# Decay times v in three wide bf16 matmuls per head, with three PSUM slots per output, in an mLSTM and gated-FFN kernel

## The chip, the cores and the metric

The kernel runs on one core of one Trainium2 chip. The metric is the device time of the kernel in microseconds, the median over runs. Names of engines: TensorE (PE) multiplies, with its weight loads listed apart (PEld); VectorE (DVE), ScalarE (ACT) and GpSimd (POOL) work on tiles; SyncE (SP) issues most transfers.

## The reference, cut to what matters

There are 4 batches of 8 heads, 768 steps and a head width of 40. Per step:

```python
m_new  = max(f + m, i);  f_stab = exp(f + m - m_new);  i_stab = exp(i - m_new)
C = f_stab * C + i_stab * outer(v, k);  n = f_stab * n + i_stab * k
y = sigmoid(o_gate) * (C @ q) / max(|n . q|, 1)
```

The 3072 rows of y (320 wide) go through a gated FFN of width 1536: `(sigmoid(x @ w_gate) * (x @ w_val)) @ w_out`.

## The kernel before, in words

The recurrence is done in 6 chunks of 128 steps. A *unit* n is one chunk c of one batch b, n = 4c + b, with all 8 heads, so there are 24 units. In a unit the scores (`s`, lines 694, 757 and 812) are multiplied by a decay matrix d (`t`, L876), and the product, 128x128 per head, is multiplied by v with a column of ones appended, 41 columns (`av`). From chunk 1 on the state's part (`in`, L918; `ti`, L923) is added. The output is then normed (`nd`, L955 to L957), gated (`ns`, L961), scaled (`ro`) and split into a high and a low part for the FFN (`xh`, `xl`). `cs`, `cd`, `cm` and `ca` (L1013 to L1056) carry the state on.

Units 0 to 7 multiply decay by v in float32 (L942). From unit 8 on, 16 units in all, both operands are split into bf16 pieces: decay into its upper half, a rest's upper half and a last rest (`da`, `db`, L891 and L895, on POOL), v likewise (`va`, `vb`, L902 and L906, on POOL). Six products of pieces are summed in PSUM:

```python
dp = top(dm[n]) if i == 0 else top(dr[n][0]) if i == 1 else dr[n][1]
vp = [top(vt[n])] if i == 2 else [top(vt[n]), top(vr[n][0]), vr[n][1]][: 3 - i]
for h in range(H):
    for j, w in enumerate(vp):
        nc.tensor.matmul(pv_[n][:, h, :], dp[:, h, :], w[:, h, :], ...)
```

That is 6 matmuls of 41 columns for each of 8 heads, 48 a unit (L935), each with its own load of decay as the weights. One VectorE instruction, `ad` (L950, 328 elements a row), then adds the state's part in place.

The FFN (`ffn`, L1064 to L1125) works through tiles of 256 or 512 columns of x. `u` and `r` (L1075, L1079, L1080) make two PSUM tiles, `pg0` and `pg1`, one buffer each. `th` and `gx` gate them, `gh` and `gl` split the result, and `dn` (L1112 to L1114) multiplies by w_out into four PSUM tiles `po`. The tiles n = 16 to 39, among them those that go with units 8 to 11, are of 256 columns.

Scores, `in`, `av`, `cs` and the transposes share two PSUM tiles, `pa0` and `pa1`, taken in turn in the order of the program (`pst`, tag "pa"). An instruction that takes one waits until everything that reads its last content is done.

The order of all work is a list written out by hand, `ORDER`. `emit` goes through it, and each engine gets its instructions in that order and keeps it. So what stands before a late instruction on its own engine is done, and what stands behind it waits. SyncE issues transfers in the same order. `wk` and `wm` (L408, L398) are matmuls on zeros that fill TensorE's time at the start.

Of the kernel before, what the change touches and what calls it, by code (L numbers as in the profile page):

```python
# [23 lines left out]
    'AV': 2,  # L24
# [7 lines left out]
    'AD': 1,  # L32
# [15 lines left out]
    i2 lf wdr0 li i3 wz tab wk0 war0 pz wk1 wk2 wk3 wdo0 ga i0 iz gm0 il sp0.0 lq2 i1 wdv0 gs0 wbr0 gb wao0 wbo0 lq0  # L48
    wav0 lk0 gc tap tac sp0.1 ee0.0 lk1 gm1 sp1.0 wco0 lq1 wcr0 ee0.1 kw0 lo0 tr0.1 wor0 whr0 wbv0 wlr0 gm2 lv0 i5
    tr0.0 sp1.1 cp0.0 cp0.1 s0.0 tr1.0 woo0 wdo4 gm3 lo1 ee1.0 ee1.1 cp1.0 wdo1 ld2 l10 tr1.1 kw1 wcv0 wov0 t0.0 lv1  # L50
    lq3 wdg0 cp1.1 wao4 tr2.0 l11 cp2.0 s1.0 who0 gm4 cs0 wlo0 wbo4 wco4 t0.1 whv0 av0 t1.0 og1 wlv0 og0 cm0.1 t1.1
    lk2 wao1 ld3 wbo1 woo4 ee2.1 who4 wco1 wlo4 woo1 wk4 av1 ee2.0 wdg1 em2 nd0 ns0 gs1 wk5 cm0.0 ro0 wk6 wdo3 wag0
    nd1 ns1 tr3.0 cp3.0 xd0 wbg0 lk3 lv2 l12 tr2.1 xt0 cp2.1 ro1 wcg0 kw2 ee3.1 wk7 xh0 wk8 who1 wk9 gm5 xd1 i8 wk10
    lo2 xt1 wdr1 wog0 xh1 xl0 wk11 xl1 wag1 ld4 wdv1 wbg1 wm gd s2.0 t2.0 t2.1 whg0 u1.0 r1.0 wlo1 tbp tbc wlg0
    tr3.1 lq4 wao3 wbo3 cp3.1 ee3.0 u0.0 r0.0 war1 og2 em3 lv3 kw3 lo3 th0 wco3 wcg1 woo3 wdo5 cs1 wbr1 cm1.1 who3
    wlo3 lk4 wog1 gx0 cm1.0 whg1 gh0 lq5 av2 ns2 ee4.0 u0.1 ee4.1 gl0 r0.1 th1 dn0.0 nd2 l13 wcr1 ro2 s3.0 wor1 t3.0
    t3.1 wlg1 u1.1 r1.1 wav1 wbv1 cs2 wcv1 wdv3 wao5 wbo5 u0.2 wov1 xd2 cm2.1 tr4.0 wco5 cm2.0 em4 cp4.0 gx1 whv1
    wlv1 whr1 wlr1 woo5 gh1 wdo2 gl1 dn0.1 og3 qb4.0 xt2 av3 ns3 dn1.1 xh2 nd3 dn1.0 u1.2 xl2 ro3 r0.2 th2 r1.2 gx2
    wao2 wbo2 xd3 tdp wco2 wdo10 tdc lk5 tr4.2 cp4.2 u0.3 gh2 r0.3 xt3 tr4.1 gl2 u1.3 r1.3 lo4 woo2 qb4.2 wao10 i6
    th3 xh3 xl3 who2 gs3 gx3 u0.4 r0.4 who5 s4.0 cp4.1 gh3 gs5 kw4 gl3 wlo5 tr5.0 wav3 t4.0 ld5 cp5.0 u1.4 r1.4  # L60
    wbo10 lv4 og4 wlo2 th4 dn2.1 dn3.1 dn2.0 dn3.0 gx4 u0.5 wbv3 ee5.0 wcv3 wco10 qb4.1 gh4 gl4 woo10 s4.2 u1.5 r0.5
    wov3 r1.5 t4.2 who10 wdv2 wlo10 whv3 dn4.2 lv5 cs3 wlv3 wdg2 th5 wag2 gx5 cm3.1 gh5 l14 wdr2 in4 wbg2 wav2 u0.6
    ti4 r0.6 gl5 cm3.0 dn5.2 wcg2 th6 wbv2 dn4.3 s4.1 wcv2 u1.6 wog2 r1.6 war2 wov2 u0.7 qb5.0 wbr2 wcr2 ee5.1 t4.1
    gx6 r0.7 whv2 wdg4 lk6 whg2 wlv2 gh6 dn5.3 gl6 em5 av4 cs4 wor2 lq6 gs4 th7 wdr3 wdg3 u1.7 r1.7 wlg2 whr2 lo5
# [33 lines left out]
    r1.32 ea11 dn31.3 gx32 gh32 gl32 u0.34 dn31.2 r0.34 tq12 lq13 tw12.3 tw12.0 tw12.1 cm9.0 tw12.2 u1.34 lo11 xw9.3
    r1.34 dn32.3 th34 gx34 u0.33 va11 r0.33 dn32.2 ee11 em11 gh34 gl34 u1.33 sh11.1 r1.33 ob1.1 sl11.0 lv12 th33
    gx33 av10.0 ld13 sl11.1 av10.1 av10.2 u0.35 xr8.1 kw11 r0.35 gh33 cd9.1 og11 gl33 ad10 xr9.0 ns10 cd9.0 s11.2  # L100
    t11.2 dn33.3 dn33.2 nd10 u1.35 r1.35 s11.0 dn34.3 t11.0 lq15 vb11 th35 gx35 dn34.2 gh35 ro10 cs10 lk13 xr9.2
    s11.1 sr12.10 ca9.1 u0.36 sr12.00 ea12 r0.36 ee12 em12 cm10.1 th36 gl35 u1.36 ca9.0 t11.1 da11 tx10 xw10.1
# [83 lines left out]
    dn102.3 ob5.3 dn102.2 ob5.2  # L186
# [11 lines left out]
def mlstm_then_gated_ffn_kernel(  # L198
# [158 lines left out]
    @op("i3")  # L357
    def _():
        block_mask(bmask, L)

    @op("i4")
    def _():
        block_mask(cmask, DA)

    @op("i5")
    def _():
        nc.gpsimd.tensor_copy(rmask, bmask[:, :, 0])
# [799 lines left out]
```

## Time and profile before

| | us |
|---|---|
| median of 3 runs | 517.56 |
| the three runs | 517.18, 517.56, 519.47 |
| the profiled execution | 516.09 |
| its span, first to last instruction | 514.3 |
| lies around the span | 1.8 |

The rows further down come from the profiled execution. A duration of one matmul (mean ns) holds its way through the array, and matmuls overlap: the pace of a stream is read from the chain of waits, where a piece of so many instructions has the length by which it moved the end on.

### The profile page before, as it was taken

What the parts mean: (1) busy time and instruction counts of PE and PEld (TensorE: products, weight loads), DVE (VectorE), ACT (ScalarE), POOL (GpSimd) and SP (SyncE); (2) the same over time, 40 slices, a digit from 0 to 9 for tenths busy, and PEclk for the clock granted to TensorE, in tenths of its full rate; (3) what the DMA queues carried; (4) which work ended last, traced back from release to release, by engine and by line L of the source; (5) the groups of instructions that cost most, each with busy time, mean ns of one, the idle gap of its engine ahead of it and who ended that gap; (6) DMA issues with size and microseconds to landing.
All of it is one profiled execution on the core that took longest, in us unless ns stands there. A gap on an engine that the chain in (4) does not pass through costs nothing.

```text
span 514.3 us, 11007 instructions
## 1 busy us (share of the span) xinstructions
PE 505.0 (98%) x4020; PEld 467.1 (91%) x4021; DVE 328.6 (64%) x699; ACT 242.4 (47%) x560; POOL 247.8 (48%) x273
## 2 busy tenths in 40 slices
PE   6999999999999999999999999999999999999997
PEld 4799988889999999998988888998888888999996
DVE  8888777775776677676766456766545474642332
ACT  4888766554444354645343543343344324233322
POOL 3656446567147687469635544287315504510000
PEclk9999999999999999999999999999999999999999
DMA  8999775339798797799879787699465735220000
GB/s 200 281 226 238 204 194 141 105 94 176 139 185 156 176 208 152 168 203 173 168 130 165 191 155 144 139 180 187 103 138 104 166 87 114 64 56 5 1 27 27
DMA packets 222478, 74.17 MB, mean 144 GB/s; under 512 B 167380, under 2 KB 214168, under 8 KB 222424
## 3 DMA queue, kind: packets, MB, share of 16 engines
q1 hardware_dynamic: 221336, 73.20, 65.3%
q8 instruction: 32, 0.52, 0.4%
q10 hardware_dynamic: 1088, 0.26, 0.2%
q14 instruction: 22, 0.18, 0.1%
HBM read 61.54 MB, written 11.90 MB: 143 GB/s over the span
## 4 chain that ended last, share of the span: by engine, by line
PE 94%; DMA 2%; ACT 2%; SPq 0%; DVE 0%; issue 0%; DVEq 0%
PE pg L1075 39%; PE po L1112 9%; PE po L1114 8%; PE po L1113 8%; PE pg L1079 7%; PE pg L1080 6%; PE av L935 4%; PE in L918 2%; PE s L757 2%; PE av L942 2%; PE cs L1018 2%; PE s L812 1%; DMA d<-mscr 1%; DMA st_v<-in_moe_w_val_dram 1%; ACT d L639 1%; PE s L694 1%
## 5 line engine op out<-in xcount | busy, mean ns | idle before, releaser
L1097 ACT ACTIVATE gh<-pg 128x256 fp32r<-128x256 f32 (+1 forms) x103 | 48.3, 469 | 141.9 <-DVE pg L1092 116.7
L1092 DVE SCALAR_TENSOR_TENSOR pg<-sg,pg 128x256 f32<-128x256 f32 (+1 forms) x103 | 54.8, 532 | 92.4 <-PE pg L1080 74.7
L1075 PE MATMUL pg<-xh,wh 128*128 128x256 f32 (+1 forms) x412 | 104.5, 334 | 0.1
L1075 PE MATMUL pg<-xh,wl 128*128 128x256 f32 (+1 forms) x412 | 100.4, 325 | 0.0
L1075 PE MATMUL pg<-xl,wh 128*128 128x256 f32 (+1 forms) x412 | 100.2, 324 | 0.0
L1112 PE MATMUL po<-oh,gh 128*128 128x320 f32 x288 | 92.8, 322 | 0.0
L1114 PE MATMUL po<-oh,gl 128*128 128x320 f32 x288 | 89.1, 309 | 0.0
L1113 PE MATMUL po<-ol,gh 128*128 128x320 f32 x288 | 88.9, 309 | 0.0
L1085 ACT ACTIVATE sg<-pg 128x256 f32<-128x256 f32 (+1 forms) x103 | 48.2, 468 | 72.6 <-PE pg L1080 71.2
L1102 DVE TENSOR_TENSOR gl<-pg,gh 128x256 fp32r<-128x256 f32 (+1 forms) x103 | 54.4, 528 | 36.6 <-ACT gh L1097 34.9
L1075 PEld LDWEIGHTS pg<-xl,wh 128*128 128x128 f32 x412 | 68.5, 188 | 7.4 <-POOL xl L1008 0.3
L1075 PEld LDWEIGHTS pg<-xh,wl 128*128 128x128 f32 x412 | 68.6, 188 | 7.1
L1075 PEld LDWEIGHTS pg<-xh,wh 128*128 128x128 f32 x412 | 67.5, 188 | 3.5 <-DVE gl L1102 0.7
L1079 PE MATMUL pg<-xh,w 128*128 128x256 f32 (+1 forms) x206 | 68.2, 332 | 0.0
L1080 PE MATMUL pg<-xl,w 128*128 128x256 f32 (+1 forms) x206 | 66.7, 324 | 0.0
L1112 PEld LDWEIGHTS po<-oh,gh 128*128 128x128 f32 x288 | 54.1, 188 | 2.8 <-ACT gh L1097 0.2
L1113 PEld LDWEIGHTS po<-ol,gh 128*128 128x128 f32 x288 | 54.2, 188 | 2.6
L1114 PEld LDWEIGHTS po<-oh,gl 128*128 128x128 f32 x288 | 54.0, 188 | 0.5 <-DVE gl L1102 0.4
L675 POOL TENSOR_SCALAR_AFFINE_SELECT d<-d 128x1024 f32<-128x1024 f32 x22 | 26.0, 1182 | 52.9 <-ACT d L671 52.1
L891 POOL TENSOR_TENSOR dr<-d 128x1024 f32<-128x1024 f32 x16 | 30.4, 1899 | 34.8 <-DVE d L876 34.4
L876 DVE TENSOR_TENSOR d<-s,d 128x384 f32<-128x384 f32 (+2 forms) x68 | 35.0, 528 | 15.8 <-PE s L757 9.2
L1080 PEld LDWEIGHTS pg<-xl,w 128*128 128x128 f32 x206 | 38.7, 188 | 2.7
(160 smaller groups left out, 883.1 us busy)
## 6 DMA issues: line engine op xcount, KB each, us to landing
d<-mscr SPq DMA_DIRECT2D x22, 512.0 KB
ks<-scq SPq DMA_DIRECT2D x48, 168.0 KB
qs<-scq SPq DMA_DIRECT2D x48, 168.0 KB
scq<-tq SPq DMA_DIRECT2D x64, 80.0 KB
su_o<-in_moe_w_out_dram SPq DMA_DIRECT2D x12, 320.0 KB
o<-in_o_gate_dram SPq DMA_DIRECT2D x24, 160.0 KB
v<-in_v_dram SPq DMA_DIRECT2D x24, 160.0 KB
out_dram<-ob SPq DMA_DIRECT2D x24, 160.0 KB
```

Of the source, the lines that this page charges most:

```text
L876: nc.vector.tensor_tensor(y, ps_[n, g][:, :nh, :], y, ALU.mult)
L891: E("da", n).tensor_tensor(dr[n][0], dm[n], top(dm[n]), ALU.subtract)
L1075: nc.tensor.matmul(p, w[y][:, a, fs], x[c][:, a, n0:n1], start=(i + a == 0), stop=False)
L1079: nc.tensor.matmul(pg[n, y], w2[y][:, fs], xh[c][:, 2, n0:n1], start=False, stop=False)
L1080: nc.tensor.matmul(pg[n, y], w2[y][:, fs], xl[c][:, 2, n0:n1], start=False, stop=True)
L1085: nc.scalar.activation(s, pg[n, 0], AF.Tanh, scale=0.5)
L1092: nc.vector.scalar_tensor_tensor(sgs[n], gate, 1.0, pg[n, 1], ALU.add, ALU.mult)
L1097: nc.scalar.activation(ghs[n][:, :nt], sgs[n], AF.Copy)
L1102: E("gl", n).tensor_tensor(gls[n][:, :nt], sgs[n], ghs[n][:, :nt].bitcast(F32), ALU.subtract)
L1112: nc.tensor.matmul(p, ghs[n][:, ts], oh[:, j, :], start=(j == 0), stop=False)
L1113: nc.tensor.matmul(p, ghs[n][:, ts], ol[:, j, :], start=False, stop=False)
L1114: nc.tensor.matmul(p, gls[n][:, ts], oh[:, j, :], start=False, stop=(j == NF - 1))
```

## The change

From unit 8 on the three pieces of v lie side by side for each head, 3 x 41 = 123 float32 words of which the upper halves are read as bf16. Decay's upper piece is multiplied by all 123 columns at once, its second by the first 82, its last by the first 41, into three slots of 41 columns of one PSUM tile for 4 heads. The slots are added afterwards by three VectorE instructions for each half of the heads (`ad`, 164 elements a row each), the last of them in PSUM, where `nd` and `ns` read, now also in halves. So the sums over the pieces of v move from PSUM's accumulation to VectorE. A new ScalarE instruction `vc` puts the upper piece of v in its place.

```diff
+            @op(f"vc{n}")
+            def _():
+                vs[n] = sbt("su", [P, H, 3, DA], F32, f"vs_{n}", 2)
+                nc.scalar.activation(top(vs[n][:, :, 0, :]), top(vt[n]), AF.Copy)
...
+                E("va", n).tensor_tensor(vs[n][:, :, 1, :], vt[n], top(vt[n]), ALU.subtract)
...
+                r = vs[n][:, :, 1, :]
+                E("vb", n).tensor_tensor(top(vs[n][:, :, 2, :]), r, top(r), ALU.subtract)
...
-                    for h in range(H):
-                        for j, w in enumerate(vp):
-                            nc.tensor.matmul(pv_[n][:, h, :], dp[:, h, :], w[:, h, :], start=(i + j + h == 0),
-                                             stop=(i == 2 and h == H - 1))
+            for y in range(2):
+                @op(f"av{n}.{y}")
+                def _(y=y):
+                    pv_[n, y] = p = pst("pa", [P, 4, 3, DA], f"av_{n}_{y}")
+                    parts = vs[n].rearrange("p h j e -> p h (j e)").bitcast(BF16)
+                    for i, (dp, w) in enumerate(((top(dm[n]), 3 * DA), (dr[n][1], DA), (top(dr[n][0]), 2 * DA))):
+                        for x in range(4):
+                            nc.tensor.matmul(p.rearrange("p x j e -> p x (j e)")[:, x, :w], dp[:, 4 * y + x, :],
+                                             parts[:, 4 * y + x, 1 : 2 * w : 2], start=(i + x == 0), stop=(i + x == 5))
+
+                for i in range(3):
+                    @op(f"ad{n}.{y}{i}")
+                    def _(y=y, i=i):
+                        t, p = t1s[n][:, 4 * y : 4 * y + 4, :], pv_[n, y][:, :, i, :]
...
+                            nc.vector.tensor_tensor(p if i == 2 else t, t, p, ALU.add)
```

Four smaller edits go with it. From unit 8 on scores and `t` come in two groups of 4 heads, not three of 3, 3 and 2:

```diff
-                for g, (h0, nh) in enumerate(GROUPS):
+                for g, (h0, nh) in enumerate(FOURS):
...
-                        ps_[n, g] = p = pst("pa", [P, 3, L], f"s_{n}_{g}")
+                        ps_[n, g] = p = pst("pa", [P, 4, L], f"s_{n}_{g}")
```

The masks `bmask` (128x384) and `cmask` are gone, and a broadcast of the 3 columns of `rmask` stands in for them; of the POOL instructions at the start, `i3` becomes that narrow and `i4` and `i5` go. Tiles of 9 heads become tiles of 8, so tiles lie at other places in SBUF. And `ORDER` is a new list: 2761 entries for 2683. Two stretches of it, the one around unit 10's `av`, and the start (entries of other engines are left out there):

```
... av10.0 sq11.0 av10.1 gx32 ad10.10 xr8.0 tw12.2 tw12.1 sh11.0 u0.34 r0.34 gh32 gl32 th34 u1.34 xw9.2 r1.34
ad10.00 vc11 dn31.3 u0.33 dn32.2 sh11.1 sl11.0 gx34 ad10.11 ea11 gh34 ca9.1 ad10.01 va11 ee11 r0.33 xw9.0 ad10.12
em11 tw12.3 ld12 dn32.3 ad10.02 gl34 sq11.1 u1.33 cd10.1 th33 xr8.2 r1.33 sl11.1 ns10.0 gx33 tw12.0 xr9.0 ob1.1
kw11 dn34.3 u0.35 gh33 nd10.0 nd10.1 ns10.1 gl33 dn34.2 s11.0 lq13 t11.0 ca9.0 s11.1

TensorE, before: s0.0 tr1.0 tr1.1 tr2.0 s1.0 cs0 av0 wk4 av1 wk5 wk6 ... xt1 wk11 wm s2.0 u1.0 r1.0
TensorE, after:  s0.0 tr1.1 tr1.0 cs0 tr2.0 wk4 wk5 av0 s1.0 wk6 tr3.0 av1 ... wm xt1 wk10 u1.0 s2.0 r1.0
SyncE, before: lf wdr0 wdo0 lq2 wdv0 gs0 lq0 lk0 lk1 lq1 lo0 lv0 wdo4 lo1 wdo1 ld2 lv1 lq3 wdg0 lk2 ld3
SyncE, after:  lf wdr0 wdo0 lv0 lq2 wdv0 gs0 lq0 lk0 lk1 lv1 lq1 lo1 wdo4 wdo1 lo0 ld2 lq3 wdg0 gs1 lk2 ld3
```

Entries: `lv` and `ld` load v and the decay's row maxima, `lq`, `lk`, `lo` the other inputs, `wd` the weights, `sl` (L737) finishes the scores' operands; `ld3` takes the buffer that `av0` reads last.

## Rows read from the trace of the kernel before

**Rows 1.** The page: busy time of each engine; clock granted in 40 slices

```profile
PE 505.0 (98%) x4020; PEld 467.1 (91%) x4021; DVE 328.6 (64%) x699; ACT 242.4 (47%) x560; POOL 247.8 (48%) x273
PEclk9999999999999999999999999999999999999999
```

**Rows 2.** Busy time by stretch: the first 40 us; the sum of 148 to 455

```profile
0.00:40.00 40.00, 34.19 (x281) 29.19 (x282) 34.18 (x90) 29.92 (x89) 21.21 (x39) 1.00 0.95 232
...
sum 307.00, PE 307.00 PEld 283.67 DVE 196.21 ACT 131.18 POOL 162.59; mean PE 76.75 PEld 70.92 DVE 49.05 ACT 32.80 POOL 40.65
```

**Rows 3.** The chain of waits: start us, length us, piece

```profile
18.12 1.77 PE av L942 x16
43.34 0.15 PE po L1112
44.49 0.12 PE pg L1079
...
148.87 1.21 PE av L935 x48
150.08 0.80 PE pg L1075 x6
152.00 0.71 PE pg L1075 x6
158.95 0.57 PE cs L1018 x6
```

**Rows 4.** The filler matmul of L408: its instructions; TensorE's timeline

```profile
L408 PE MATMUL pkeep<-warm x11: 379/379/631, 2.8 to 25.5; 128*128 128x512 bf16 x11
...
24.14 1.03 PE L408 MATMUL pkeep<-warm 128*128 128x512 bf16 x4
```

**Rows 5.** TensorE's weight loads by line, shapes apart: count, busy us, mean ns

```profile
L942 PEld LDWEIGHTS av<-v,d 128*128 128x128 f32 x128 | 15.1, 192 | 0.0
L935 PEld LDWEIGHTS <-d 128*128 128x128 bf16 x384 | 11.7, 98 | 0.4 <-issue 0.3
L408 PEld LDWEIGHTS <-warm 128*128 128x128 bf16 x12 | 1.4, 126 | 3.5 <-issue 2.0 <-DVE warm L293 1.3
```

**Rows 6.** VectorE's instructions by line, shapes apart: count, busy us, mean ns

```profile
L1092 DVE SCALAR_TENSOR_TENSOR pg<-sg,pg 128x512 f32<-128x512 f32 x41 | 28.4, 692 | 41.5 <-PE pg L1080 30.4 <-issue 4.3 <-ACT ob L1123 3.6
L1092 DVE SCALAR_TENSOR_TENSOR pg<-sg,pg 128x256 f32<-128x256 f32 x62 | 26.5, 427 | 50.8 <-PE pg L1080 44.3 <-ACT sg L1085 3.5 <-issue 1.8
L737 DVE SCALAR_TENSOR_TENSOR ks<-ks,rsign,kt 126x1024 fp32r<-126x1024 f32 x16 | 20.5, 1281 | 2.6 <-ACT kt L731 1.3 <-DMA scx<-tx 1.2
L1056 DVE TENSOR_TENSOR cst<-cst,ct 120x246 f32<-120x246 f32 x16 | 11.0, 688 | 1.9 <-ACT ct L1048 1.9
L950 DVE TENSOR_TENSOR av<-t,av 128x328 f32<-128x328 f32 x20 | 10.0, 500 | 4.3 <-PE av L935 3.9 <-PE av L942 0.2
L1056 DVE TENSOR_TENSOR cst<-cst,ct 80x82 f32<-80x82 f32 x16 | 6.4, 400 | 0.6 <-ACT ct L1048 0.5
L955 DVE TENSOR_SCALAR den<-av 128x8 f32<-128x8 f32 x24 | 3.8, 160 | 0.3
```

**Rows 7.** VectorE's timeline: two instructions of 256 elements, one behind the other

```profile
172.64 0.42 DVE L876 TENSOR_TENSOR d<-s,d 128x256 f32<-128x256 f32 x1
172.98 0.42 DVE L1102 TENSOR_TENSOR gl<-pg,gh 128x256 fp32r<-128x256 f32 x1
```

**Rows 8.** ScalarE's instructions by line: the copy nearest to the added one

```profile
L910 ACT ACTIVATE o<-o 128x320 f32<-128x320 f32 x24 | 11.0, 463 | 1.4 <-DMA o<-in_o_gate_dram 1.4
```

**Rows 9.** The start: the chain's pieces, and SyncE's timeline of one issue

```profile
3.58 5.22 DMA st_v<-in_moe_w_val_dram
16.28 1.09 PE s L694 x16
19.95 5.37 DMA d<-mscr
...
13.00 0.43 SPq L609 DMA_DIRECT2D v<-in_v_dram  x1
```

More of the change, by code (lines that the diff above doesn't have):

```diff
@@ L47 @@
 ORDER = """
[L48 to L52, printed above, removed]
@@ L98 @@
[L98 to L102, printed above, removed]
@@ L183 @@
[L183 to L186 removed]
+    i2 lf wdr0 li i3 wz tab wk0 war0 pz wk1 wk2 wk3 wdo0 ga i0 iz lv0 gm0 l10 il sp0.0 lq2 i1 wdv0 gs0 wbr0 gb wao0
+    wbo0 lq0 wav0 lk0 gc tap tac sp0.1 ee0.0 lk1 gm1 tr0.1 gm2 sp1.0 wco0 lv1 tr0.0 gm3 gm4 sp1.1 l11 lq1 wcr0 ee0.1
@@ new lines @@
+    wbv0 gm5 lo1 cp0.1 wor0 wcv0 woo0 cp0.0 whr0 ee1.0 wdo4 s0.0 wov0 wdo1 tr1.1 who0 cp1.1 lo0 ld2 lq3 wlr0 tr1.0
+    kw0 t0.0 whv0 cs0 cp1.0 ee1.1 tr2.0 wao4 wlo0 t0.1 wdg0 cm0.1 cp2.0 wbo4 wao1 kw1 wco4 woo4 wk4 cm0.0 wlv0 og0
+    wk5 av0 og1 s1.0 who4 wbo1 nd0 wk6 tr3.0 ee2.0 ee2.1 t1.0 cp3.0 wco1 t1.1 ns0 av1 ro0 woo1 gs1 wk7 lk2 xd0 tr2.1
+    wlo4 wag0 ld3 lv2 nd1 xt0 wbg0 wdg1 wk8 lk3 ns1 wcg0 xh0 em2 ro1 lo2 who1 cp2.1 ee3.1 xd1 wdo3 wk9 wm xt1 kw2
+    xh1 wdr1 wk10 l12 xl0 wog0 whg0 wag1 lv3 gd ee3.0 wlg0 xl1 u1.0 s2.0 wlo1 i8 r1.0 ld4 l13 wbg1 wdv1 wao3 em3
@@ L264, in mlstm_then_gated_ffn_kernel @@
     m0 = sbt("t1", [P, L], F32, "m0", 2)
-    sel = sbt("t1", [P, P], F32, "sel", 2)
+    sb.tile([P, L], F32, tag="t11", name="t11_first")
     gin = sb.tile([BH, 2, S], F32, tag="xh0", name="gin")
@@ L274, in mlstm_then_gated_ffn_kernel @@
     mend = const.tile([BH, NCH + 1], F32, name="mend")
-    bmask = const.tile([P, 3, L], F32, name="bmask")
-    cmask = const.tile([P, 3, DA], F32, name="cmask")
     rmask = const.tile([P, 3], F32, name="rmask")
-    ones = bmask[:BH, 0, :]
+    ones = rmask[:BH, 0:1].broadcast_to([BH, L])
     ident = const.tile([P, P], F32, name="ident")
@@ L286, in mlstm_then_gated_ffn_kernel @@
     cst = const.tile([P, B, 3, 3 * DA], F32, name="cst")
+    sel = sb.tile([P, P], F32, tag="qk1", name="sel")
     late = sb.tile([P, L], F32, tag="qk0", name="late") if PARAM["MP"] else None
@@ L925, in unit @@
         if halved:
[L926 to L936 removed]
+            for y in range(2):
[10 more added lines that the diff above has]
+                    def _(y=y, i=i):
+                        if n not in t1s:
+                            t1s[n] = sbt("t1", [P, H, DA], F32, f"t1_{n}", 2)
+                        t, p = t1s[n][:, 4 * y : 4 * y + 4, :], pv_[n, y][:, :, i, :]
+                        if c == 0 and i == 0:
+                            nc.scalar.activation(t, p, AF.Copy)
+                        else:
+                            nc.vector.tensor_tensor(p if i == 2 else t, t, p, ALU.add)
         else:
@@ L942, in _ @@
                     nc.tensor.matmul(p[:, h, :], dm[n][:, h, :], vt[n][:, h, :], start=True, stop=True)
-        def hs():
-            return t1s[n] if c > 0 and not PARAM["AD"] else pv_[n]
-        if c > 0:
+        if c > 0 and not halved:
             @op(f"ad{n}")
             def _():
-                nc.vector.tensor_tensor(hs(), t1s[n], pv_[n], ALU.add)
-        @op(f"nd{n}")
-        def _():
-            rden[n] = den = sbt("den", [P, H], F32, f"den_{n}", 2)
-            nc.vector.tensor_scalar(den, hs()[:, :, D], -2.0, 2.0, ALU.mult, ALU.max)
-            nc.vector.scalar_tensor_tensor(den, hs()[:, :, D], 2.0, den, ALU.mult, ALU.max)
-            nc.vector.reciprocal(den, den)
-        @op(f"ns{n}")
-        def _():
-            nc.vector.scalar_tensor_tensor(ot[n], ot[n], 1.0, hs()[:, :, :D], ALU.add, ALU.mult)
+                nc.vector.tensor_tensor(pv_[n], t1s[n], pv_[n], ALU.add)
+        for y in range(2 if halved else 1):
+            hs = (lambda y=y: pv_[n, y][:, :, 2, :]) if halved else lambda: pv_[n]
+            heads = slice(4 * y, 4 * y + 4) if halved else slice(0, H)
+            yn = f"{n}.{y}" if halved else f"{n}"
+            @op(f"nd{yn}")
+            def _(hs=hs, heads=heads):
+                if n not in rden:
+                    rden[n] = sbt("den", [P, H], F32, f"den_{n}", 2)
+                den = rden[n][:, heads]
+                nc.vector.tensor_scalar(den, hs()[:, :, D], -2.0, 2.0, ALU.mult, ALU.max)
+                nc.vector.scalar_tensor_tensor(den, hs()[:, :, D], 2.0, den, ALU.mult, ALU.max)
+                nc.vector.reciprocal(den, den)
+            @op(f"ns{yn}")
+            def _(hs=hs, heads=heads):
+                o = ot[n][:, heads, :]
+                nc.vector.scalar_tensor_tensor(o, o, 1.0, hs()[:, :, :D], ALU.add, ALU.mult)
         @op(f"ro{n}")
@@ L1044, in _ @@
                 tmps[y] = tmp
-                if is_act("cm", n):
-                    for j in range(w // DA):
-                        js = slice(j * DA, (j + 1) * DA)
-                        nc.scalar.activation(tmp[:, :, js], pc_[n][:r, gs, js], AF.Copy, scale=rmask[:r, j : j + 1])
-                else:
-                    cm = cmask.rearrange("p j e -> p (j e)")[:r, :w].unsqueeze(1).broadcast_to([r, ng, w])
-                    nc.vector.tensor_tensor(tmp, pc_[n][:r, gs, :w], cm, ALU.mult)
+                for j in range(w // DA):
+                    js = slice(j * DA, (j + 1) * DA)
+                    nc.scalar.activation(tmp[:, :, js], pc_[n][:r, gs, js], AF.Copy, scale=rmask[:r, j : j + 1])
             if c > 0:
```

310 lines of the change are left out of this document (151 added, 159 removed).

## The prediction, made before the changed kernel was run

> **What bounds the kernel now.** First the page: TensorE is busy 98% of the span, VectorE 64%, ScalarE and POOL under half, and the granted clock is full in every slice [rows 1], that is the 2.4 GHz level. Then the busy times by stretch: of the first 40 us TensorE misses 5.8, but from 148 to 455 us, where units 8 to 23 run, its 307.0 us of 307.0 are all busy, while VectorE has 196.2, 64% [rows 2]. So in that stretch only TensorE's own stream counts, and what leaves it comes off the end. Last the chain of waits, for the length of each piece: a block of 48 matmuls of L935 moves the end on by 1.21 us, 25.2 ns each, and the FFN piece right behind it takes 0.80 us where the same piece elsewhere takes 0.71 [rows 3]. That 0.09 is the price of going from bf16 back to float32, paid once for each run of bf16 blocks.
>
> **TensorE's part, the main term.** Before, 16 units x 48 x 25.2 ns = 19.4 us. After, each of 8 heads has one matmul of 123 columns, one of 82 and one of 41: the same 246 columns, in 3 matmuls and weight loads rather than 6. What does a wide bf16 matmul with its own weight load cost? The nearest rows are the filler matmuls of 512 columns: one lasts 379 ns, and four in a row last 1.03 us in the timeline, so one follows the other after (1.03 - 0.379) / 3 = 217 ns [rows 4]. Each has a load of its own, 12 in all [rows 5]. 512 columns at 2.4 GHz are 213 ns, so some 3 ns are fixed, and the load is hidden. By the same rule 123 columns take 51.3 + 3 = 54 ns and 82 take 34.2 + 3 = 37; 41 stay at 25.2, which is not 17 + 3, hence a floor. A unit is 8 x (54 + 37 + 25.2) = 0.93 us. It saves 0.28, and 16 units save **4.5 us**.
>
> The ends: with nothing fixed the two wide ones take 51 and 34 ns, a unit 0.88 us, a saving of 5.3 in all. On a straight line from (41 columns, 25.2 ns) to (512, 217), 0.41 ns a column, they take 59 and 42, a unit 1.01 us, a saving of 3.2. The far end is the float32 block, 1.77 us for 16 matmuls of 41 columns, 111 ns each whatever their width [rows 3]: with 111, 111 and 25 a unit would take 1.98 us and the kernel lose 12. I put it aside, since a bf16 load lasts 98 ns and a float32 one 192 [rows 5], and 48 bf16 loads already pass within 1.21 us.
>
> The bf16 blocks stood in 17 runs on TensorE and stand in 16, since in the new list both halves of each unit's `av` are neighbours there: 0.1 us saved. Scores have the same 128 matmuls in fewer groups: nothing.
>
> **VectorE's part.** A line through 256 elements at 427 ns and 512 at 692 gives 0.16 us fixed and 1.03 ns an element; it puts 328 elements at 0.50, as the row of `ad` has it [rows 6]. So an `ad` of 164 takes 0.33, and six for one add 1.5 us a unit. `ns` in halves adds 0.16, `nd` another three small instructions at 0.16 [rows 6], 0.5; `t` in two groups of 512 for 384, 384 and 256 gives back 0.15. Some 2.0 us a unit, 32 in all: VectorE goes from 64 to 74% of the middle. Under TensorE's 307 us that costs nothing by itself. What is late next is the output's PSUM tile: before, `ad`, `nd` and `ns` give it back after 1.5 us, now three adds, `nd` and `ns` for each half, among the FFN's `gx` and `gl` and the scores' `sl`. Unit 10 is the tightest. From `av10.1` to `s11.1`, which takes the same tile, TensorE has five `u` at 0.71, four `r` at 0.24, five `dn` at 0.45 and four score matmuls at 0.11: 7.2 us [rows 3]. From its first add to its last reader VectorE has six `ad`, two `sl` at 1.28, four `gx` or `gl` at 0.43, one `ca` at 0.40, two `ns` at 0.32 and two `nd` at 0.48: 8.3 [rows 6]. TensorE would wait 1.1. Counted so, units 8 and 9 come to 0.5 and 0.1, the others to none: 1.7 us. But the timeline has 0.34 us from one instruction of 0.42 to the next [rows 7]; with 0.08 off for each of the 21, unit 10 needs 6.6, and nothing waits. Before, the tightest was unit 13, 1.5 us against 1.8, and TensorE did not wait. Between 0 and 1.7 I take **0.6 us lost**.
>
> **The start.** `s1.0`, 1.09 us, stood ahead of `av0`, and `av0` releases the buffer of the transfer that then ends the wait for 5.37 us [rows 9]; in the new list it stands behind. Against it `lv0` is issued ahead of `wdv0` on SyncE, 0.43 us, and `wdv0` is the transfer of 5.22 us on the chain [rows 9]. Transfers share the queue, which may swallow either: between 1.1 gained and 0.6 lost, I take **0.5 gained**. `i3`, `i4` and `i5` shrink on POOL, off this path: nothing, and nothing to be lost either, as the scan that reads the mask waits for its transfer.
>
> **Beside TensorE.** `vc` is a ScalarE copy of 328 elements like the one at 463 ns [rows 8], 7.4 us in all; behind it stand `gh` and `th`, covered while ScalarE is half idle [rows 1]; without that cover a unit could lose up to 0.46. `va` and `vb` write other places on POOL at the same counts; that they or other tiles lie elsewhere in SBUF is taken at nothing, as no row shows a price of a place.
>
> **The sum.** -4.5 - 0.1 + 0.6 - 0.5 = -4.5 us. The profiled execution took 516.09, span 514.3 and 1.8 around it, which gives 511.6; the median of the runs stands 1.47 above it, so 513.1. A measurement of this kernel can tell about 0.5%, 2.6 us, from no change; -4.5 is 0.9%.
>
> **The rivals.**
>
> *The weight load is not hidden behind a short stream.* 25.2 ns may be the load's own pace. If load and stream then follow each other, 123 columns take 51 + 25 = 76 ns, 82 take 59, a unit 8 x (76 + 59 + 25.2) = 1.28, 0.07 more than before, 1.1 in all, and the kernel stays at 518.7. For it: the 98 ns of a load exceed the stream of 123 columns. Against it: the filler's loads cost 3 ns, and 41 columns then would not fit in 25.2. Chance 0.08. The Trainium skill, in "TensorE: Matmul & The Clock Gate", section "Back-to-back issue gap", speaks for this rival: a sustained stream of load and matmul pairs goes at about 81 ns for 128 columns, more than the array time. On a line from the row's 25.2 ns at 41 columns to that figure a unit would come to 1.24 us, an estimate by that page, no gain. The filler's row does not agree with it, but shows 512 columns only.
>
> *The output's PSUM tile is given back too late: slower.* The place is `s` or `in` behind `av`. The state's add of 82 elements takes 400 ns and that of 246 takes 688 [rows 6], 1.76 ns an element; if `ad` went like that, 164 would take 0.54, unit 10 would wait 2.4, and units 8, 9, 13, 16 and 18 some 1.8, 1.4, 1.3, 0.4 and 0.7: 8.0 us, and the kernel takes 521. From 7.1 us of such waits, 0.44 a unit, it is slower by more than 0.5%. For it: VectorE at 74%, and counts so close to TensorE's. Against it: those two rows have both operands in SBUF, and `ad` has its own row. Chance 0.10. Half of that, some 4 us, leaves 516 to 517, within 0.5%: chance 0.14.
>
> *The new order also mends the start.* TensorE misses 5.8 us of the first 40 [rows 2]; should the whole of the 1.1 and another us go, 511. Chance 0.06.
>
> **How the numbers follow.** The forecast, 511.5 to 514.9, has 0.62, the better start 0.06: faster 0.68. Half the waits, 0.14, and the load that shows, 0.08: same 0.22. Slower 0.10. The range starts from 513.1. Down to 510.2 it takes in 0.8 more from the matmuls (5.3 for 4.5), no wait (0.6), the full 1.1 at the start (0.6) and 0.9 of spread, less than lies between any of the three runs and the profiled execution. Up to 517.3 it takes in the straight line (1.3), nothing at the start (0.5) and 3 us of waits for 0.6 (2.4). It leaves out the slower rival, most of the load's and a little below.
>
> **What would show it.** In the chain, a unit's 24 matmuls at 0.93 us, once 0.09 behind them; 1.28 says the load shows, 1.01 the straight line. `ad` at 0.33 and VectorE at 74% between 148 and 455 us, TensorE without a wait there; waits of `s` or `in` for VectorE's `ns` or `nd` are the slower rival, and I am wrong if they pass 2 us. In the start, `ld3`'s transfer issued before 19.9 us. If the blocks shrink by 4.5 us and the time does not, the order lost it elsewhere.

## The result, and the profile after

The changed kernel takes 521.75 us in the median (520.02 to 523.65); the kernel before, measured again beside it, 517.23 (516.74 to 519.47). The ratio is 1.0085, with a 95% interval of 1.0057 to 1.0113: 4.5 us slower, where 4.5 us faster was forecast. The profiled execution of after took 523.65 us, span 521.9, and is the slowest of its six runs: its span is 7.6 us above that of before, where the medians are 4.5 apart, so what stages differ by below is more than the medians would give.

First the page: busy time of each engine, and the clock granted in 40 slices, which answer to [rows 1].

```profile
PE 508.4 (97%) x3634; PEld 465.7 (89%) x3637; DVE 353.9 (68%) x827; ACT 248.0 (48%) x576; POOL 240.0 (46%) x269
...
PEclk8899999999999999999999999999999999999999
```

TensorE has 386 matmuls fewer and is yet busy for 3.4 us more, and the clock is no longer full in the first two slices. The busy times by stretch answer to [rows 2] and show where (columns as there: the stretch, its length, PE, PEld, DVE, ACT and POOL busy, granted clock, DMA share, GB/s).

```profile
0.00:40.00 40.00, 31.93 (x224) 26.69 (x227) 30.13 (x74) 24.26 (x69) 15.14 (x34) 0.91 0.85 210
...
148.00:455.00 307.00, 305.86 (x2183) 279.12 (x2182) 215.19 (x499) 138.91 (x285) 163.28 (x157) 1.00 0.76 152
```

Of the first 40 us TensorE misses 8.1 instead of 5.8, at 0.91 of the clock instead of 1.00. To put a figure on each stage, both spans are cut where the FFN has reached the same place: at the start of the 12th, the 46th and the 168th matmul of `r`'s second kind (L1080 before, L1090 after), called FFN events from here on. Units 8 to 23 lie between the 46th and the 168th. All kernels of this study stand in the table (us, each from its profiled execution, but for the last column).

| kernel | to 12th event | 12th to 46th | 46th to 168th | rest | median of runs |
|---|---|---|---|---|---|
| before | 54.7 | 92.4 | 307.9 | 59.4 | 517.2 |
| after | 62.0 | 92.3 | 308.0 | 59.6 | 521.75 |
| e1 | 57.0 | 92.3 | 308.0 | 59.6 | 517.96 |
| e2 | 58.0 | 92.3 | 307.8 | 59.5 | 519.39 |
| e3 | 61.3 | 92.3 | 307.5 | 59.5 | 521.65 |
| e4 | 55.6 | 92.0 | 336.3 | 60.5 | 545.32 |
| e5 | 60.0 | 92.3 | 310.3 | 59.6 | 525.38 |
| e6 | 60.2 | 92.7 | 306.6 | 59.6 | 521.89 |
| e7 | 59.1 | 92.3 | 307.7 | 59.6 | 520.32 |
| e8 | 59.5 | 92.1 | 309.7 | 59.4 | 521.23 |
| e9 | 62.0 | 92.3 | 306.8 | 59.8 | 520.86 |
| e10 | 55.4 | 92.3 | 307.0 | 59.6 | 516.21 |
| e11 | 55.2 | 93.0 | 307.5 | 59.8 | 518.06 |
| e12 | 55.7 | 92.7 | 306.8 | 59.6 | 516.43 |

Work other than the FFN's is not cut quite alike: by the 12th event the changed list has done six `in` matmuls, 0.6 us, that the list before has not (so have e1 to e3, e5 to e7 and e9), and in its middle stand six `in` fewer and six of `dn` more, which take the same time. So two things need an explanation: 7.3 us more pass before the 12th event, 6.7 of them lost, and the middle, where 4.5 us were to be saved, saves nothing.

**The matmuls.** In the chain of waits of after, a unit's 24 matmuls are pieces of about 1.01 us, against 1.21 to 1.23 for 48 [rows 3]. The 16 blocks with what follows them come to 16.1 us for 19.7 (from the start times of all matmuls of the middle): 3.5 us are saved.

```profile
172.41 1.01 PE av L933 x24
...
189.74 1.02 PE av L933 x24
```

**The start.** The longest waits of TensorE for work of this kernel (us in total, times, longest us); in the timelines behind them stand start us and busy us, and in brackets the idle time before and what ended it.

```profile
PE pt L763 <- DMA pad<-in_k_dram: 2.8, 1, 2.8
PE pg L1085 <- DVE gl L1112: 1.3, 2, 1.1
```

Before, the first scores came at 12.93 us and k was issued at 5.01 us:

```profile
12.93 1.16 PE L694 MATMUL s<-qkt 40*128 40x128 f32 x16 [0.18 <-ACT qkt L774]
```

```profile
5.01 1.13 SPq L604 DMA_DIRECT2D pad<-in_k_dram  x2
```

The timeline of TensorE after, from 7 us:

```profile
7.22 1.05 PE L627 MATMUL mb<-m,ident 128*128 128x128 f32 x8
11.06 1.11 PE L763 MATMUL pt<-ident,pad 128*128 128x128 f32 x4 [2.79 <-DMA pad<-in_k_dram]
11.97 0.63 PE L624 MATMUL mb<-late,ident 128*128 128x512 bf16 x1
12.40 1.91 PE L627 MATMUL mb<-m,ident 128*128 128x128 f32 x8
...
15.39 1.86 PE L627 MATMUL mb<-m,ident 128*128 128x128 f32 x8
17.18 1.16 PE L691 MATMUL s<-qkt 40*128 40x128 f32 x16
```

SyncE's timeline after:

```profile
3.12 0.43 SPq L606 DMA_DIRECT2D v<-in_v_dram  x1
...
6.41 1.16 SPq L601 DMA_DIRECT2D pad<-in_k_dram  x2
7.61 2.47 SPq L606 DMA_DIRECT2D v<-in_v_dram  x1
...
24.02 0.34 SPq L651 DMA_DIRECT2D d<-mscr  x1
```

The new list issues the first load of v ahead of those of k, which go out at 6.41 us, and has the transposes of k (`tr0.1`, L763) ahead of the next mask block (`sp1.0`, L627). TensorE keeps the order: it stands idle for 2.8 us, with `sp1.0` ready behind. Then eight mask matmuls take 1.9 us for the 1.05 of the block at 7.22. The granted clock is 0.52 between 10 and 15 us and 0.79 in the next 5, which means the 1.2 GHz level for nearly all of the first and some two fifths of the second; before, both slices had 1.00. The first scores come at 17.18 us instead of 12.93, and the transfer that stood at 19.95 [rows 9] is issued at 24.02.

### The profile page after: what moved, and what is told of

Read it like the earlier page. It is cut to its first block, busy times and chain, and to the rows that moved or that the text cites. A ratio compares the mean times of both kernels' runs of the same rounds, so it can differ in the third digit from the quotient of the medians.

```text
span 521.9 us, 10408 instructions
## 1 busy us (share of the span) xinstructions
PE 508.4 (97%) x3634; PEld 465.7 (89%) x3637; DVE 353.9 (68%) x827; ACT 248.0 (48%) x576; POOL 240.0 (46%) x269
## 4 chain that ended last, share of the span: by engine, by line
PE 91%; DVE 3%; DMA 2%; SPq 1%; ACT 1%; issue 1%; DVEq 0%; ACTq 0%
PE pg L1085 38%; PE po L1122 8%; PE po L1124 8%; PE po L1123 8%; PE pg L1089 6%; PE pg L1090 6%; PE av L933 3%; PE s L754 3%; PE in L918 2%; PE av L951 2%; PE cs L1032 2%; DMA k<-in_k_dram 2%; PE s L809 1%; DMA pad<-in_k_dram 1%; PE s L691 1%
## 5 line engine op out<-in xcount | busy, mean ns | idle before, releaser
L1090 PE MATMUL pg<-xl,w 128*128 128x256 f32 (+1 forms) x206 | 66.6, 325 | 0.0
L664 POOL TENSOR_TENSOR d<-at,d 128x1024 f32<-128x1024 f32 x16 | 31.5, 1969 | 20.8 <-DMA d<-mscr 20.8
L1089 PEld LDWEIGHTS pg<-xh,w 128*128 128x128 f32 x206 | 38.7, 188 | 2.3
```

What stands on the lines that cost most here:

```text
L664: E("ea", n).tensor_tensor(dm[n], a, dm[n], ALU.subtract)
L1089: nc.tensor.matmul(pg[n, y], w2[y][:, fs], xh[c][:, 2, n0:n1], start=False, stop=False)
L1090: nc.tensor.matmul(pg[n, y], w2[y][:, fs], xl[c][:, 2, n0:n1], start=False, stop=True)
```

## The experiments

Each starts from the changed kernel unless it says otherwise.

**e1, the start alone.** The old list up to `u1.0`, then the rest of the new one.

```diff
 ORDER = """
-    i2 lf wdr0 li i3 wz tab wk0 war0 pz wk1 wk2 wk3 wdo0 ga i0 iz lv0 gm0 l10 il sp0.0
+    i2 lf wdr0 li i3 wz tab wk0 war0 pz wk1 wk2 wk3 wdo0 ga i0 iz gm0 il sp0.0 lq2
...
```

> The changed kernel, with the entries of the list up to the first FFN matmuls (u1.0) in the order of the kernel before; behind them the changed list as it is. Theory S, the whole loss arises at the start: the first u1.0 comes at about 29.5 us rather than 34.5, the granted clock is full between 10 and 20 us, and the time falls by 6 to 7.5 us, to 514 to 516. Rival M, the new order of the middle or the other places in SBUF cost as much as the start: the start is mended, but the time stays at or above 517.

517.96 us, ratio to before 1.0017 (0.9990 to 1.0044). The 12th event moves from 62.0 to 57.0 us, the wait for k and the low clock are gone, and the middle stays at 308.0. So 5.0 of the 7.3 us lie in the entries up to `u1.0`. The 514 to 516 of theory S is missed, since the middle saves nothing: in time it is rival M.

**e2, one entry of TensorE.**

```diff
-    gm1 tr0.1 gm2 sp1.0 wco0
+    gm1 gm2 sp1.0 tr0.1 wco0
```

> The changed kernel with one entry moved: tr0.1 behind sp1.0, so that on TensorE the matmuls of sp1.0, whose inputs are there, no longer stand behind the transposes that wait for k. Theory S1, the place on TensorE decides: the wait of 2.8 us for k is cut to about 1.5, TensorE is not idle for as long before it, the clock stays at 2.4 GHz, 4 us or more come back: at most 518. Theory S2, the late transfer of k decides: s0.0 still starts at about 17 us, and the time falls by less than 2 us, to about 520.

519.39 us, 1.0037 (1.0015 to 1.0058): about half of the loss, from one entry, between the two theories (518 and 520). The clock stays full in every slice of the start, and the first scores come at 13.02 us, as before the change. The wait for k shrinks to 0.9, but a later one appears:

```profile
PE cs L1027 <- POOL k L877: 1.4, 1, 1.4
...
PE pt L758 <- DMA pad<-in_k_dram: 0.9, 1, 0.9
```

**e3, the loads of v.** `lv0`, `lv1` and what belongs to them go back behind the loads of q and k on SyncE.

```diff
-    ga i0 iz lv0 gm0 l10 il
+    ga i0 iz gm0 il
...
-    sp1.0 wco0 lv1 tr0.0 gm3 gm4 sp1.1 l11 lq1
+    sp1.0 wco0 tr0.0 gm3 gm4 sp1.1 lq1
...
-    wbv0 gm5 lo1 cp0.1
+    wbv0 gm5 lo1 lv0 l10 cp0.1
...
-    lo0 ld2 lq3
+    lo0 ld2 lv1 l11 lq3
```

> The changed kernel with lv0 and lv1 back behind the loads of q, k, o and the first weights (and their memsets l10, l11 behind them). Theory S2: k is issued at about 5.0 us rather than 6.4 and lands at 9.5 rather than 11.0, s0.0 starts some 3 us earlier and 4 us or more come back: at most 518. Theory S1: TensorE still waits with sp1.0 behind the transposes, the clock still falls, and at most 2 us come back: about 520.

521.65 us, 1.0085 (1.0050 to 1.0119): no gain. But the timelines of SyncE and TensorE show that the wait at `tr0.1` is gone:

```profile
5.03 1.07 SPq L596 DMA_DIRECT2D pad<-in_k_dram  x2
```

```profile
9.48 0.66 PE L758 MATMUL pt<-ident,pad 128*128 128x128 f32 x4 [0.81 <-DMA pad<-in_k_dram]
...
12.73 1.16 PE L686 MATMUL s<-qkt 40*128 40x128 f32 x16
...
16.40 0.83 PE L1027 MATMUL cs<-v,k 128*120 128x123 f32 x6 [1.48 <-POOL k L877]
...
26.58 1.09 PE L758 MATMUL pt<-ident,pad 128*128 128x128 f32 x4 [1.96 <-DMA pad<-in_k_dram]
```

k is issued and met as theory S2 has it, TensorE waits 0.8 us for it, as in the kernel before, the clock stays full up to 20 us, and the first scores come at 12.73. What S2 has wrong is that this brings time back. The loss arises again behind the scores: `cs` waits 1.5 us for POOL's k, the transposes at 26.58 wait 2.0 us for a later load of k, and the clock is at 0.50 between 25 and 30 us. So the first wait needs both moves, and the changed list's start loses time in other places too.

**e4, the wide matmuls in the old order.** The changed code with the old list: each old entry of scores, `av`, `ad`, `nd` and `ns` is replaced by the new ones at its place, some drawn ahead so that a PSUM tile's readers precede its next use. For one half of unit 20 the gate is applied before its tanh is taken, so that half is not the reference's.

```diff
-    in12 av12.0 av12.1 sh13.1
+    in12 sh13.1
...
-    tw14.1 av12.2 gl44
+    tw14.1 av12.0 ti12 av12.1 gl44
```

> The changed kernel's code (three wide matmuls, three slots, scores in fours) in the order of the list before; vc stands ahead of va, av.0 and av.1 where av.2 stood, the adds, nd and ns where ad, nd and ns stood, and a few readers are drawn ahead of the next user of their PSUM tile. Theory W, the wide matmuls give 3.5 us (1.01 us a unit for 1.23) and little of it is lost: 513.5 to 515.5. Rival T, the output's PSUM tile is given back too late in an order not made for it: waits of in, s or cs for ns or nd in the trace, and 517 or more.

545.32 us, 1.0529 (1.0481 to 1.0576). The start is as before (55.6 us), and the middle is 28.4 us longer; the waits between 140 and 460 us begin so:

```profile
PE s L749 <- issue: 5.5, 5, 2.8
PE av L928 <- DVE d L868: 3.5, 4, 1.5
PE pg L1080 <- DVE gl L1107: 2.3, 4, 0.9
```

The time is rival T's, but of T's waits the trace names one alone, 0.7 us of `s` for `nd`. One `av` now takes two of the PSUM tiles that were taken in turn, and the old order was not made for that: this is the likely reason, and not shown. The run says that a new list was needed, and nothing on what a wide matmul is worth. The next one does.

**e5, the narrow matmuls in the new order.**

```diff
                         for x in range(4):
-                            nc.tensor.matmul(p.rearrange("p x j e -> p x (j e)")[:, x, :w], dp[:, 4 * y + x, :],
-                                             parts[:, 4 * y + x, 1 : 2 * w : 2], start=(i + x == 0), stop=(i + x == 5))
+                            for j in range(w // DA):
+                                nc.tensor.matmul(p[:, x, j, :], dp[:, 4 * y + x, :],
+                                                 parts[:, 4 * y + x, 2 * j * DA + 1 : 2 * (j + 1) * DA : 2],
+                                                 start=(i + x + j == 0), stop=(i + x == 5 and j == w // DA - 1))
```

> The changed kernel, its list untouched; only each wide bf16 matmul (123, 82 or 41 columns) is cut into matmuls of 41 columns again, into the same PSUM slots, 48 a unit. Theory W (the wide matmuls are worth what the trace shows, 42.0 ns x 24 against 25.6 x 48, and the order has eaten it): a unit takes 1.23 us for 1.01, 16 units 3.5 us more, so 525.3 against 521.75 for the changed kernel. Rival T (TensorE was never the end in the middle; something else, VectorE or a transfer, paces it in the new order): under 1 us more, 521.7 to 522.7.

525.38 us, 3.6 us above the changed kernel: theory W. Its blocks in the chain:

```profile
170.28 1.24 PE av L934 x48
...
187.84 1.24 PE av L934 x48
```

With 16 x (1.24 - 1.01) = 3.7 us the wide matmuls keep what the trace gives them. The middle grows by 2.3 only, since here the wait of 1.1 us for `gl` does not come up.

**e6, the parts of v in a row.** So that a moving row is read at every element.

```diff
-                vs[n] = sbt("su", [P, H, 3, DA], F32, f"vs_{n}", 2)
-                nc.scalar.activation(top(vs[n][:, :, 0, :]), top(vt[n]), AF.Copy)
+                vs[n] = sbt("su", [P, 3 * H * DA], F32, f"vs_{n}", 2)
+                z = vs[n][:, : 3 * H * DA // 2].bitcast(BF16).rearrange("p (h j e) -> p h j e", j=3, e=DA)
+                nc.scalar.activation(z[:, :, 0, :], top(vt[n]), AF.Copy)
...
+                nc.scalar.activation(z[:, :, 1, :], top(r), AF.Copy)
+                E("vb", n).tensor_tensor(z[:, :, 2, :], r, top(r), ALU.subtract)
...
-                                             parts[:, 4 * y + x, 1 : 2 * w : 2], start=(i + x == 0), stop=(i + x == 5))
+                                             parts[:, 4 * y + x, :w], start=(i + x == 0), stop=(i + x == 5))
```

> The changed kernel, its list untouched; the three bf16 parts of v lie in a row of their own, so that a moving row is read at every element and not at every second one; it costs one more ScalarE copy of 328 elements a unit, about 0.46 us, 7.4 us in all beside other work. Theory C (the step of two slows the wide matmuls): 123 columns fall from 61 to 54 ns, 82 from 40 to 37, a unit from 1.01 to 0.93, 16 units 1.2 us less: 520.5. Rival F (each matmul pays 7 to 10 ns of its own besides its columns): 61 and 40 ns as before, and 521.7, or up to 0.5 more where the copy stands ahead of the FFN's on ScalarE.

521.89 us. Both theories have a part: 123 columns go from 61.4 to 58.2 ns (mean, from start to start), 82 from 40.6 to 36.4, and 41 stay. A unit takes 0.96 to 0.97 us, 0.8 us less in all, not 1.2. In its execution the wait of TensorE for `gl` is gone and one of 0.7 us before an `av` has come (the added ScalarE copy ends 0.10 us before that `av` starts), so the total shows nothing.

```profile
170.72 0.96 PE av L937 x24
...
187.94 0.97 PE av L937 x24
```

**e7, filler in the wait.**

```diff
+    @op("wf")
+    def _():
+        zeros = warm.bitcast(BF16)
+        for _ in range(12):
+            nc.tensor.matmul(keep[0], zeros[:, :P], zeros[:, :NT], start=True, stop=True)
...
-    gm1 tr0.1 gm2 sp1.0
+    gm1 wf tr0.1 gm2 sp1.0
```

> The changed kernel with 12 more filler matmuls of 512 bf16 columns (217 ns each, 2.6 us) ahead of tr0.1 on TensorE, where it waits 2.8 us for k. They compute nothing that is used. Theory G (the idle stretch brings the granted clock down to 0.52 between 10 and 15 us, and the eight mask matmuls of two blocks take 1.7 us for 0.9): the clock stays at 1.00, k is met as late as before, and the 12th FFN event falls from 61.96 to about 59.0; 518.8. Rival H (the time is lost in the wait itself and in what k's lateness moves, the clock only fills idle time): 521.5 to 522.

520.32 us, 1.0051 (1.0024 to 1.0078), between the two. The stretches from 5 to 15 us:

```profile
5.00:10.00 5.00, 5.00 (x27) 3.78 (x26) 4.63 (x12) 1.06 (x3) 0.00 (x0) 1.00 1.10 247
10.00:15.00 5.00, 5.00 (x44) 4.02 (x43) 4.03 (x12) 3.98 (x14) 0.64 (x1) 1.00 1.00 194
```

The clock stays full though k comes no earlier, and the 12th event is at 59.1 us, as theory G has it; the first scores come at 14.32 us. Four kernels here have the changed list's start untouched, and it goes differently in each execution:

| | wait for k | clock from 10 to 15 us | first scores | 12th event |
|---|---|---|---|---|
| after | 2.8 | 0.52 | 17.18 | 62.0 |
| e9 | 3.0 | 0.51 | 17.27 | 62.0 |
| e6 | 2.1 | 0.67 | 15.81 | 60.2 |
| e5 | 1.8 | 1.00 | 14.19 | 60.0 |

In e5 the clock fell later, to 0.66 between 25 and 30 us. Against 59.1 the low clock costs 0.9 to 2.9 us at the 12th event. The other 4.4 us are not k's lateness alone: with a full clock the scores are 1.4 us late (14.32 for 12.93). Of the rest, 0.6 are the `in` matmuls, and some 2.4 arise behind the scores, as they do in e2, whose scores are on time and whose 12th event is 3.3 us late.

**e8, the kernel before with the two moves.** From the kernel before.

```diff
-    il sp0.0 lq2 i1
+    il sp0.0 lv0 lq2 i1
...
-    sp1.0 wco0 lq1 wcr0 ee0.1 kw0 lo0 tr0.1
+    tr0.1 sp1.0 wco0 lv1 lq1 wcr0 ee0.1 kw0 lo0
...
-    gm2 lv0 i5
+    gm2 i5
...
-    t0.0 lv1 lq3
+    t0.0 lq3
```

> The kernel before, with two of the new list's moves alone: lv0 and lv1 far ahead on SyncE, ahead of the loads of q and k, and tr0.1 ahead of sp1.0 on TensorE. Theory S (these two make the start's loss): TensorE waits over 2 us for k, the granted clock falls below 0.7 in a slice of 5 us between 10 and 20 us, and the kernel takes 4 to 5 us more, 521.5 to 522.5. Rival M (the loss needs the rest of the new start): within 1.5 us of the kernel before, 517.2 to 518.7.

521.23 us, 1.0072 (1.0042 to 1.0102): 3.6 us more than the 517.67 of the kernel before beside it, just under theory S's 521.5. The wait and the clock are the ones of after:

```profile
PE pt L761 <- DMA pad<-in_k_dram: 3.1, 1, 3.1
```

and by stretch:

```profile
10.00:15.00 5.00, 3.79 (x17) 3.64 (x18) 3.56 (x8) 3.16 (x11) 2.28 (x3) 0.50 1.13 229
15.00:20.00 5.00, 4.75 (x39) 4.06 (x37) 2.30 (x6) 4.00 (x12) 1.22 (x5) 0.83 0.95 271
```

So the two moves make 4.9 us by the 12th event, of the 6.7 that are lost, without any of the new code. Its runs go with their mean granted clock: the three at 1.000 took 517.82, 518.30 and 519.86 us, the six at 0.990 to 0.993 took 520.52 to 523.86. Likewise e3's two at 1.000 took 519.24 and 519.47, its three at 0.987 to 0.993 took 522.49 to 525.09. So most of these moves' price comes with the low clock; whether k also came sooner in the runs at full clock, no trace shows. Its middle is 1.9 us longer too, 0.6 of it in waits of scores; the rest stays open.

**e9, one entry of VectorE in the middle.** The one wait over 0.7 us in the middle of after is `pg` for `gl`, at 311.9 us. VectorE's timeline there:

```profile
309.71 2.90 DVE L734 SCALAR_TENSOR_TENSOR qs<-qs,rsign,qt 126x1024 fp32r<-126x1024 f32 x1
312.54 0.68 DVE L1112 TENSOR_TENSOR gl<-pg,gh 128x512 fp32r<-128x512 f32 x1
```

and POOL's:

```profile
309.63 1.90 POOL L664 TENSOR_TENSOR d<-at,d 128x1024 f32<-128x1024 f32 x1 [8.45 <-DMA d<-mscr]
311.49 2.88 POOL L888 TENSOR_TENSOR dr<-d 128x1024 f32<-128x1024 f32 x1
```

The split of q takes 2.90 us, for a median of 1.28, and `gl` stands behind it.

```diff
-    r0.58 vc17 lq20 sl17.0 va17 gl57
+    r0.58 vc17 lq20 gl57 sl17.0 va17
```

> The changed kernel; in its list only gl57 is moved, from behind the split of q of unit 17 (sl17.0) to ahead of it. Theory P (the one wait over 0.4 us of the middle, 1.1 us of pg for gl at 311.9 us, comes from this split standing ahead of gl57 on VectorE and lasting 2.9 us for its usual 1.28, while POOL runs a 1.90 us subtraction that began 0.08 us earlier): the wait goes, the middle between the 46th and the 168th FFN event falls from 308.0 to 306.8, the kernel by 1.2 us to 520.5. Rival Q (VectorE is behind by then as a whole, and the split put later makes the scores of unit 17 or the next tile wait instead): the wait comes back within 10 us under another name, 521.3 to 522.

Theory P to the tenth: the middle is 306.8 us and holds no wait of 0.2 us or more. The kernel takes 520.86 us, 0.9 less than the changed one; as the runs of the two overlap (519.80 to 522.57, 520.02 to 523.65), it is the trace that shows the gain.

**e10 to e12, versions that join what was found.** e10 has the old list up to `u0.19`, the new one behind it, and `gl57` ahead; e11 the same with the old list up to `u1.6` only; e12 is e10 with the parts in a row of e6.

```diff
 ORDER = """
-    i2 lf wdr0 li i3 wz tab wk0 war0 pz wk1 wk2 wk3 wdo0 ga i0 iz lv0 gm0 l10 il sp0.0
+    i2 lf wdr0 li i3 wz tab wk0 war0 pz wk1 wk2 wk3 wdo0 ga i0 iz gm0 il sp0.0 lq2
...
-    r0.58 vc17 lq20 sl17.0 va17 gl57
+    r0.58 vc17 lq20 gl57 sl17.0 va17
```

> The changed kernel with the old list up to u0.19 (some 137 us, the first 8 units, whose operations the change does not touch), the new list behind it, and gl57 ahead of sl17.0. Theory S (the whole loss of 7.3 us lies in the new list's first 55 us, the wide matmuls are worth 3.5 us, and the new list's middle gives that back in waits and switches): the 12th FFN event is at 54.7 as before, the middle is 306.8, and the kernel takes 1.1 us less than before, 516.3. Rival M (the splice makes waits of its own, since entries of units 8 and 9 now come late): the stretch from the 46th event on is longer by over 1 us, 517.5 or more.

516.21 us for 516.3 expected, 0.9977 (0.9956 to 0.9998): just faster than the kernel before, and 5.5 us below the changed one. This is theory S. The middle is 307.0, the 12th event at 55.4, not 54.7; in this execution the clock fell to 0.67 between 20 and 25 us.

```profile
20.00:25.00 5.00, 4.95 (x29) 4.26 (x30) 3.83 (x15) 4.12 (x13) 3.07 (x4) 0.67 1.04 261
```

> As the run before it, but the old list only up to u1.6 (some 62 us). Theory S: the 12th FFN event at 54.7, the middle 306.8, 516.3, the same as with the longer prefix, since the two lists cost the same between the 12th and the 46th event (92.4 and 92.3 us). Rival M: the shorter prefix disturbs less behind it and is faster by over 0.5 us than the longer one, or the new list leans on the early part of its own, and it is slower by as much.

518.06 us, 1.0008 (0.9989 to 1.0027): the shorter piece is the worse, as the second half of rival M has it: by 0.8 us between the 12th and the 46th event and 0.6 in the middle. Where one list hands over to the other has its own price.

> As e10, and the three bf16 parts of v in a row of their own as in e6. There 123 columns took 58.2 ns for 61.4 and 82 took 36.4 for 40.6, and 16 units 0.8 us less. Theory C: 0.8 us less than e10, 515.5, clearly faster than the kernel before by 0.3 to 0.5%. Rival F: the extra copy on ScalarE (0.46 us a unit) puts a wait of av or gh on TensorE, as the 0.7 us that e6 shows at av, and the gain goes: as e10 or slower.

516.43 us, 0.9973 (0.9955 to 0.9990): faster than the kernel before, but not than e10. The 0.7 us that the blocks save come back in a wait, as rival F has it; it is put down to no releaser, but here too the added ScalarE copy ends 0.10 us before that `av` starts:

```profile
PE av L932 <- issue: 0.7, 1, 0.7
```

These three have the changed code, with its tiles at other places in SBUF, behind the old list's start, and reach the 12th event at 55.2 to 55.7 us: the code and the places cost about 1 us at most there, the low clock of e10 included.

## Why the prediction was wrong

**The start, the step that failed most.** The prediction took 0.5 us gained, from two moves: `s1.0` behind `av0` and `lv0` ahead of `wdv0`. It priced `lv0` by `wdv0` and not by k, which goes out 1.4 us later for it, and it never asked what a third move, `tr0.1` ahead of `sp1.0`, puts in front of a ready block on TensorE. Either of the two taken back brings the first scores back to their place (e3, e2). The step lost 6.7 us in the profiled execution, for a forecast range of 1.1 gained to 0.6 lost: 4.2 ahead of the first scores, where the wait and the low clock stand, and 2.4 behind them, which the old list's start gives back but for 0.8 (e10) and whose entries were not singled out. e1 gives back 5.0 of it, e2 with one entry 4.0, and e8 takes 4.9 from the old kernel by the two moves alone. By medians, e10 against the changed kernel less the 1.2 us of its `gl57`, the start costs 4.3 us. The test it named, `ld3`'s transfer before 19.9 us, came out at 24.0. The chain of before showed a wait of TensorE for k of 0.8 us at that place: what stood in it was the transfer, and any work that could be done meanwhile had to stay in front.

**The wide matmuls, a sound mechanism a little mis-sized.** 123, 82 and 41 columns take 61, 41 and 26 ns, which is the straight line through the two rows (59, 42, 25.2), its far end and not the 54 and 37 taken. A unit takes 1.01 us for 0.93, and the term is 3.5 us for 4.5, inside its bounds of 3.2 and 5.3. e6 shows that the step of two makes 3 to 4 ns of each and some 7 ns remain fixed on 123 columns, where the filler's 512 showed 3. The rival of a load that shows is out: 1.01 and not 1.28. The figure of the Trainium skill ("TensorE: Matmul & The Clock Gate", section "Back-to-back issue gap"), 81 ns for a pair of 128 columns, is not borne out either for bf16 here, with 61 ns at 123.

**The middle, "nothing waits", with the tile mistaken.** Against -3.5 us stand about 3.6 that the new order and VectorE cost:

- Waits for `gl`. The output's PSUM tile, on which 0.6 us (0 to 1.7) and the slower rival rested, made no wait that the trace shows. It was the FFN's: seven `u` tiles begin 54 to 56 ns behind the end of a `gl`, so it released them; before, none comes closer than 125 ns. The waits are 1.6 us together, 1.25 of it the one that e9 removes, and behind each the second `u` matmul is 103 to 111 ns late, 0.75 in all; three of the seven stand behind `cs` or `av`, where 84 ns of it come in any case (the third item), which leaves 0.5. VectorE's added work is 25.3 us over the span (328.6 to 353.9), less than the 32 counted, and 70% of the middle, not 74%; but `gl` now stands behind work that it did not stand behind before. The counts were made for `ad`, `nd` and `ns` alone.
- Scores, costed at nothing. The first matmul of a run of scores is followed after 60 ns, the others after 111. The same 120 matmuls in fewer runs take 0.7 us more.
- Runs of one kind. The second FFN matmul behind a run of scores is 52 ns late, behind one of `in`, `cs` or `av` 84. The prediction counted runs of `av` only (17 to 16, right). Runs of scores fall from 30 to 19, those of `in` and `cs` rise from 16 to 27: 0.3 us more.

The sum is -3.5 + 1.6 + 0.5 + 0.7 + 0.3 = -0.4, measured +0.15; the other 0.5 us are in smaller shifts of the FFN's matmuls, and what makes them stays open. The first item is shown by e9 in its largest part; the others are read from start times, and no run changed them.

**What was right.** The blocks shrink, TensorE sets the end of the middle (e5: what its blocks take comes off or on the end), `ad` takes 0.32 to 0.33 us, `vc` and `i3` cost nothing that shows. The prediction's last sentence, that the order lost it elsewhere if the blocks shrink and the time does not, names the case. The chance of 0.10 for slower was put on one mechanism in the middle and none on the start.

## What to carry to other kernels

When a list of work is ordered anew, go through each engine's first thirty instructions and ask of each pair that changed places what the one in front waits for: one entry that waits for a transfer ahead of a ready block cost here, by e2, 4.0 us in the profiled executions and 2.4 by the medians, about what dropping 384 matmuls saved (3.5). Where a change loads an engine off the path, count the buffers that every other user of that engine gives back, not only those of the new instructions. And measure a change of code within the new order, by putting the old code there, since old order and new code need not fit.

## What the hardware showed that was not expected

**A wait that costs twice.** Behind 2.8 us of idle TensorE the granted clock was at 0.5 for several us, and 12 useless matmuls in the gap kept it at 1.00 (e7). The same start gave 62.0 and 60.0 us at the 12th event in different executions; even with the old start the clock fell in the profiled executions of e10, e11 and e12, to 0.67, 0.66 and 0.66 between 20 and 25 us.

**VectorE held by POOL.** The split of q (two operands in SBUF) that began 0.08 us behind a POOL subtraction ended 1.08 us after that subtraction's end (311.53, 312.61). In e9 it began 1.25 us behind it and again ended 1.08 us after its end (311.64, 312.72). VectorE's row in e9, and POOL's:

```profile
310.99 1.73 DVE L729 SCALAR_TENSOR_TENSOR qs<-qs,rsign,qt 126x1024 fp32r<-126x1024 f32 x1
```

```profile
309.74 1.90 POOL L659 TENSOR_TENSOR d<-at,d 128x1024 f32<-128x1024 f32 x1 [8.05 <-DMA d<-mscr]
```

The Trainium skill, in "SBUF — State Buffer", section "SBUF: two separate sides", says that VectorE and GpSimd share a pair of ports that one instruction holds for its whole length, so that the other waits; a VectorE instruction with two operands in SBUF, against a GpSimd one that reads SBUF, is among them. Both timelines agree, and so do the other splits: of the 32 in after, five take over 1.4 us, and each of them ends 1.08 us after the end of a POOL instruction that began ahead of it; the other 27 take 1.27 to 1.29. The trace of before has two such, of 1.41 and 2.09 us. In the prediction this would have told which of VectorE's 1.28 us may become 2.90.
